# An attention and feed-forward kernel: the tail's exponentials turned through DRAM together with the fourth tile's, decay tiles spread by VectorE from a table, Q and K in one load

## The chip, the core and the metric

One core of a Trainium2 chip runs the whole program in one launch. The metric is the device time of one execution in microseconds (us); lower is better. Three executions of the kernel before are given, and one execution was profiled.

## What is computed

The reference is causal attention with a multiplicative decay, for 8 batches and 8 heads of 576 positions and width 64, and behind it a feed-forward layer of width 2048 with a leaky activation. All is in float32.

```
scores = scale * q @ k^T                       # (8, 8, 576, 576)
cum    = cumsum(log(clip(f, 1e-4, 1)), -1)
scores = where(causal, -1e9, scores + cum[..., :, None] - cum[..., None, :])
attn   = exp(scores - max);  attn = attn / (sum(attn) + 1e-9)
x      = (attn @ v) reshaped to (4608, 512)
h      = x @ w_in                              # (4608, 2048)
out    = where(h > 0, h, alpha * h) @ w_out    # (4608, 512)
```

## The kernel before

**Pairs.** The attention goes over 32 pairs n (8 batches, 4 pairs of heads each). A pair has four query tiles of 128 rows, called tile 0 to 3, for each of its two heads, and a *tail*: the last 64 queries of both heads, stacked as one tile of 128 rows by 576 keys. For each piece TensorE makes the scores (`stretch` L604, `tail` L526), VectorE adds the decay and takes the row's minimum (L639, L541), ScalarE takes the exponentials and their sums (L508).

**Turning.** The product with V needs the exponentials with keys on partitions. Tiles 0 to 2 are turned by TensorE: a transposition of 128 by 128 (`blocks` L521) into a PSUM bank, then a copy into an `eT` buffer (L516, L517). The tail is turned the same way: four blocks (L548), two copies of 256 columns (L551) and one more block of 64 columns (L677, L684). Tile 3 is turned so in the pairs below 8. From pair 8 on (`NX`, L30), in the 24 pairs that the code calls *turned*, tile 3 of both heads is stored to DRAM (`ex`, L659), read back by four loads that put the key's 32-row blocks where they belong (`em`, L660), and turned in 32 by 32 blocks by two VectorE instructions (L665) into `eT3`. The last 64 key rows of `eT3` come in another order than V has, so a second copy of V in that order (`vs`, L497) is loaded for them. The product with V (`prods_of` L687) runs behind the scores of tile 2 of the pair that follows.

**Decay tiles.** `Z` and `Zt` hold the cumulated decay of the two heads, the same on every partition. Except for pair 0 they are loaded from DRAM with a broadcast over partitions: two loads of 256 KB and two of 144 KB a pair (L443, L463). GpSimd then adds the causal mask (L447 to L449, L464).

**Splitting.** From pair 4 on (`NN`), Q and K are split by ScalarE and GpSimd into high and low parts (L472, L473) for products in three terms. `w_in` is split in 16 pieces by `split64` (L306) on ScalarE, VectorE and GpSimd, through the buffers `wr` and `wa`.

**Feed-forward.** `ffn1` (L783) makes the hidden layer of one batch as soon as the four pairs of that batch are done: 192 matmuls of 512 columns a batch, 9 batches in all (the tails make the ninth). They fill TensorE between the pieces of attention; in each, ScalarE and VectorE empty the bank (L803, L805) and a store puts it to DRAM. `ffn2` (L951) follows at the end with seven products for eight.

**What sets the order.** The program makes a list of operations with engine, estimated time, key and buffers; `Plan.run` (L115) plays them through a model of the engines once, while the kernel is built, and issues them in that order. On the chip each engine goes through its list in this fixed order. All DMAs but two at the end are issued by SyncE (SP), in its own fixed order. The model takes a DMA's channel time as its KB over 280 (L160).

## Time and profile before

| what | value |
|---|---|
| three executions | 1069.55, 1071.41, 1076.15 us (median 1071.41) |
| the profiled execution, its own time | 1073.41 us |
| its span in the profile | 1071.6 us |
| mean granted TensorE clock | 0.992 |
| busy: TensorE, weight loads | 1054.9, 916.7 us |
| busy: VectorE, ScalarE, GpSimd | 738.6, 675.0, 280.5 us |
| the last block transposition of the attention (L665) starts at | 580.4 us |

PE is TensorE's matmul row, PEld its weight loads, DVE is VectorE, ACT ScalarE, POOL GpSimd, SPq SyncE's queue of DMAs. Rows that group instructions give the line, the engine, the operation, what it writes and reads, the shape and the count, and behind the bar the busy time in us, the mean duration in ns, and the idle time of the engine before them with what ended it. PEclk is the granted clock of TensorE in tenths. PE durations overlap, since matmuls are pipelined: what one costs is read from the start of one to the start of the next.

### The profile page before, as it was taken

Reading aid. Unit: us, or ns where it says so; the run is one execution under the profiler, and the core shown is the slowest. Engines: PE = TensorE matmul, PEld = TensorE weight load, DVE = VectorE, ACT = ScalarE, POOL = GpSimd, SP = SyncE. Lnnn points to the kernel's source line nnn. Section 1 sums busy time; section 2 is a strip of 40 time slices with the busy share of each in tenths; the row PEclk is TensorE's granted clock in tenths of the full one; section 3 lists DMA queues with packets and bytes.
Section 4 is the critical chain, followed back from the end, with each engine's and each line's share of the span. In section 5 each row is a group of like instructions: output and inputs, shape, how many; then the busy total and the mean of one; then the engine's idle time right before and its main releaser. Section 6 shows DMA issues by size and latency. Waiting matters only on the chain.

```text
span 1071.6 us, 22543 instructions
## 1 busy us (share of the span) xinstructions
PE 1054.9 (98%) x8132; PEld 916.7 (86%) x8132; DVE 738.6 (69%) x1680; ACT 675.0 (63%) x1590; POOL 280.5 (26%) x407
## 2 busy tenths in 40 slices
PE   8889989999999999999999999999999999999998
PEld 5678867888888888888788888899999999999998
DVE  6788864555544545545544599779988898989994
ACT  6879877786766766667655375656454554646551
POOL 6578574553433434344221000000000000000000
PEclk9989999999999999999999999999999999999999
DMA  6967778987887986886763666464444443444411
GB/s 181 268 194 235 225 217 232 271 264 238 253 237 214 259 241 203 242 247 212 215 198 129 204 214 225 167 199 139 136 126 132 137 137 120 138 130 126 140 60 40
DMA packets 152441, 202.15 MB, mean 189 GB/s; under 512 B 18930, under 2 KB 89481, under 8 KB 152329
## 3 DMA queue, kind: packets, MB, share of 16 engines
q1 hardware_dynamic: 152041, 200.51, 61.3%
q8 instruction: 64, 1.05, 0.4%
q14 instruction: 48, 0.39, 0.1%
q10 hardware_dynamic: 288, 0.20, 0.1%
HBM read 139.55 MB, written 61.11 MB: 187 GB/s over the span
## 4 chain that ended last, share of the span: by engine, by line
PE 92%; DMA 2%; POOL 2%; DVE 1%; issue 1%; ACT 1%; SPq 0%; DVEq 0%; POOLq 0%
PE bank L332 86%; PE bank L521 5%; DMA Z<-c 2%; PE bank L392 1%; POOL Z L447 1%; DMA wr<-in_w_in_dram 0%; POOL wi L328 0%; POOL Z L448 0%; PE bank L677 0%; DVE eT L516 0%; DVE wa L322 0%; POOL Z L449 0%; ACT e L508 0%; POOL Ql L473 0%; POOL Kl L473 0%
## 5 line engine op out<-in xcount | busy, mean ns | idle before, releaser
L332 PE MATMUL bank<-xx,wi 128*128 128x512 f32 x1728 | 428.4, 397 | 2.3 <-ACT wi L327 1.8
L332 PEld LDWEIGHTS bank<-xx,wi 128*128 128x128 f32 x1728 | 314.4, 188 | 68.7 <-issue 4.8
L805 DVE SCALAR_TENSOR_TENSOR hs<-bank,sa,hs 128x512 f32<-128x512 f32 x96 | 71.2, 743 | 109.9 <-ACT hs L803 109.8
L332 PE MATMUL bank<-wot,xx 128*128 128x256 f32 x1008 | 123.9, 283 | 0.0
L332 PE MATMUL bank<-wi,xx 128*128 128x256 f32 x1008 | 123.9, 283 | 0.0
L332 PEld LDWEIGHTS bank<-wot,xx 128*128 128x128 f32 x1008 | 122.3, 192 | 0.0
L332 PEld LDWEIGHTS bank<-wi,xx 128*128 128x128 f32 x1008 | 122.3, 192 | 0.0
L508 ACT ACTIVATE e<-e,st 128x512 f32<-128x512 f32 (+2 forms) x160 | 109.2, 685 | 4.2 <-DVE st L541 2.0
L803 ACT ACTIVATE hs<-bank,ab 128x512 f32<-128x512 f32 x96 | 66.0, 688 | 63.4 <-PE bank L332 62.6
L517 ACT ACTIVATE eT<-bank 128x384 f32<-128x384 f32 (+2 forms) x192 | 83.3, 461 | 34.7 <-PE bank L332 20.1
L725 POOL TENSOR_TENSOR xx<-xs,xx 128x256 fp32r<-128x256 f32 x64 | 49.0, 783 | 136.6 <-ACT xx L723 136.4
L473 POOL TENSOR_TENSOR Ql<-rq,Qh 128x640 fp32r<-128x640 f32 x28 | 45.1, 1611 | 137.8 <-ACT Qh L472 89.7
L332 PE MATMUL bank<-eT,vr 128*64 128x128 f32 (+2 forms) x1408 | 80.0, 263 | 0.2 <-DVE eT L516 0.2
L332 PEld LDWEIGHTS bank<-eT,vr 128*64 128x64 f32 x1408 | 63.9, 138 | 14.1 <-issue 7.1
L447 POOL TENSOR_TENSOR Z<-Z,tri 128x384 f32<-128x384 f32 x64 | 60.0, 945 | 45.5 <-DMA Z<-c 31.2
L999 ACT ACTIVATE xx<-gx 128x1024 fp32r<-128x1024 f32 x48 | 50.8, 1058 | 30.8 <-PE bank L332 15.1
L521 PEld LDWEIGHTS bank<-ident,e 128*128 128x128 f32 x384 | 46.9, 146 | 20.5 <-issue 5.3
L521 PE MATMUL bank<-ident,e 128*128 128x128 f32 x384 | 62.2, 287 | 1.9 <-DVE st L639 1.6
L1002 DVE TENSOR_TENSOR xx<-gx,xx 128x1024 fp32r<-128x1024 f32 x48 | 58.6, 1220 | 7.4 <-ACT xx L999 7.4
L332 PE MATMUL bank<-wi,gh 128*128 128x256 f32 x504 | 62.4, 283 | 0.0
L332 PE MATMUL bank<-wot,gh 128*128 128x256 f32 x504 | 62.4, 283 | 0.0
L332 PEld LDWEIGHTS bank<-wot,gh 128*128 128x128 f32 x504 | 61.4, 192 | 0.1
(140 smaller groups left out, 1777.6 us busy)
## 6 DMA issues: line engine op xcount, KB each, us to landing
hd<-hs SPq DMA_DIRECT2D x144, 256.0 KB
wx<-hd SPq DMA_DIRECT2D x47, 512.0 KB
Z<-c SPq DMA_DIRECT2D x62, 256.0 KB
hr<-hd SPq DMA_DIRECT2D x25, 512.0 KB
ex<-e SPq DMA_DIRECT2D x24, 512.0 KB
em<-ex SPq DMA_DIRECT2D x96, 128.0 KB
rq<-in_qq_dram SPq DMA_DIRECT2D x32, 320.0 KB
vr<-in_vv_dram SPq DMA_DIRECT2D x32, 320.0 KB
```

What stands on the lines that cost most here:

```text
L332: pe.matmul(o, lhsT, rhs, start=start, stop=stop)
L392: op("PE", 800, lambda: [pe.matmul(bw.t, wbf[:, 0:128], wbf, start=True, stop=True) for _ in range(3)], -200, [o_wbf], [bw])
L447: m1 = op("POOL", c_po(128 * 3), lambda z4=z4: po.tensor_tensor(z4()[:, 6:9], z4()[:, 0:3], tb(3), ALU.add), kc + 0.1, got + [o_mask], [bZ])
L473: o2 = op("POOL", c_po(w), lambda hi=hi, lo=lo, raw=raw: po.tensor_tensor(lo(), raw.t, hi().bitcast(F32), ALU.subtract), kc, [o1], [raw, bQ])
L508: ex = op("ACT", c_exp(w), lambda: ac.activation(at(bt.t)[:, :w], at(bt.t)[:, :w], AF.Exp, bias=lo()[:, col : col + 1], scale=-1.0, accum_ ...
L517: return op("ACT", c_act(w), lambda: ac.activation(dst(), src(), AF.Copy), key, deps, [bank] + bufs)
L521: pe.transpose(t[:, c : c + 128], src[:, 128 * j : 128 * j + 128], ident)
L725: xl = op("POOL", c_po(256), lambda r=r, t0=t0: po.tensor_tensor(bx.t[:, 1, t0 : t0 + 256], bxs[r].t[:, 0:256], bx.t[:, 0, t0 : t0 + 256]. ...
L803: cp = op("ACT", c_act(512), lambda bh=bh, bs=bs, fc=fc: ac.activation(bs.t, bh.t, AF.Relu, scale=ab[:, fc : fc + 1]), -1000, [last, o_sg] ...
L805: cp = op("DVE", c_dve(512), lambda bh=bh, bs=bs, fc=fc: ve.scalar_tensor_tensor(bs.t, bh.t, sa[:, fc : fc + 1], bs.t, ALU.mult, ALU.add), ...
L999: his.append(op("ACT", c_acs(128 * GW * (j1 - j0)), lambda j0=j0, j1=j1, src=src, o_=o_: ac.activation(o_(0, j0, j1), src(), AF.Copy), key ...
L1002: rdy.append(op("DVE", c_dve(128 * GW * (j1 - j0)), lambda j0=j0, j1=j1, src=src, o_=o_: ve.tensor_tensor(o_(1, j0, j1), src(), o_(0, j0, ...
```

## The change

Three things are done together.

1. **Turned pairs** are now 9 to 31. In them the tail's exponentials are written behind tile 3's in the same buffer, go to DRAM with them in one store (768 KB), come back in the same four loads (12 blocks in place of 8 each), and are turned by two more VectorE instructions. `eT3` has a row of 192 columns for each head and block: 128 of tile 3 and 64 of the tail, so four V matmuls a head of 192 columns take the place of four of 128 and four of 64. The tail's four TensorE transpositions and two copies are gone in these pairs; its last block of 64 columns stays. V comes as one load of eight blocks (`vt`) in place of `vv` and `vs`. Pair 8 turns its tile 3 by TensorE again.
2. **Decay tiles** of pairs 10 to 31 (`NZ`) are no longer loaded. After `w_in` is split, its buffers are free: the 64 rows of the cumulated decay are loaded there once, turned by four VectorE instructions into a table with positions on 32 partitions, copied to the other 96 partitions by six DMAs, and sorted by GpSimd. From the table, two VectorE instructions a pair (1024 and 576 columns) write `Z` and `Zt`, with the same value repeated over 32 columns at their source, so that the turned block has it on every partition. `em` lies in the same memory, and can be used only once the table is made.
3. **Q and K** are one tensor, loaded by one DMA of 608 KB from pair 4 on. The planner's model takes 220 in place of 280 for a DMA's channel time in its first 90 us.

The diff, cut to its core:

```diff
-NX = (8, B * NP)
+FAR = 90.0
+NX = (9, B * NP)
+NZ = 1+9
+NQ = 4
...
-                self.chan = max(self.chan, s + 1.4) + o.kb / 280.0
+                self.chan = max(self.chan, s + 1.4) + o.kb / (220.0 if s < FAR else 280.0)
...
-    rT3 = ring(sp, 1, [128, 2, 4, 128], F32, "eT3_")
-    rm3 = ring(sp, 1, [128, 8, 128], F32, "em")
+    rT3 = ring(sp, 1, [128, 4, 384], F32, "eT3_")
+    wr = sp.tile([128, 1280], U64, name="wr")
+    wf = wr.bitcast(F32)
+    rm3 = Ring(Store([]))
+    em = wf[:, 0:1536].rearrange("p (k s) -> p k s", s=128)
...
-        l_q = op("SP", 450, lambda: sy.dma_start(bq.t, qq[b, p]), kq, dq, [bq], kb=320)
-        l_k = op("SP", 450, lambda: sy.dma_start(bk.t, kk[b, p]), kq, dq, [bk], kb=288)
+        l_qk = [op("SP", 450, lambda c0=c0, c1=c1: sy.dma_start(bqk.t[:, c0:c1], qk[b, p][:, c0:c1]), kq, dq, [bqk], kb=(c1 - c0) / 2)
+                for c0, c1 in (((0, QW), (QW, QW + S)) if n < NQ else ((0, QW + S),))]
...
+        if spread:
+            def rows_of(src, k):
+                return src.rearrange("p s (h o) -> p h s o", o=1).broadcast_to([128, k, src.shape[1], 32])
+
+            zz = op("DVE", c_tr(1024), lambda: ve.transpose(
+                Z()[:, :, 0:512].rearrange("p h (s c) -> p h s c", c=32), rows_of(cq[:, 0:16, 2 * n : 2 * n + 2], 2)), kl + 4, [o_cq], [bZ])
+            zt = op("DVE", c_tr(S), lambda: ve.transpose(
+                Zt().rearrange("p (s c) -> p s c", c=32), rows_of(ct[:, :, n : n + 1], 1)[:, 0]), kl + 4.1, o_ct, [bZ])
...
-            nt = expo(bt, S, 4, st + 0.6, [prev])
+            nt = expo(bt, S, 4, st + 0.6, [prev], tail_of)
+            if turned:
+                return bt, nt
...
-                o_ = op("SP", 400, lambda: sy.dma_start(d.rearrange("h q k -> q h k"), b3.t), key, [be[0][3][1], nm], [b3], kb=512)
+                o_ = op("SP", 400, lambda: sy.dma_start(d.rearrange("g q k -> q g k"), b3.t[:, 0:1536].rearrange("p (g k) -> p g k", g=3)),
+                        key, [be[0][3][1], nm, nt], [b3], kb=768)
...
+                for g in range(3):
+                    def turn(g=g):
+                        o = bT3.t[:, :, 192 * g : 192 * g + 128].rearrange("p s (a c) -> p a s c", a=4) if g < 2 else None
+                        if g < 2:
+                            ve.transpose(o, bm.t[:, 4 * g : 4 * g + 4].rearrange("p a (s r) -> p a s r", r=32))
+                        else:
+                            for h_ in range(2):
+                                ve.transpose(bT3.t[:, :, 192 * h_ + 128 : 192 * h_ + 192].rearrange("p s (a c) -> p a s c", a=2),
+                                             bm.t[:, 8 + 2 * h_ : 10 + 2 * h_].rearrange("p a (s r) -> p a s r", r=32))
...
+    o_cl = op("SP", 400, lambda: sy.dma_start(cl, c8), kc_, [o_c8] + [o for v in w_ready.values() for o in v], kb=147)
...
+    o_qc = [op("SP", 400, lambda a=a, c=c: sy.dma_start(c[32 * a : 32 * a + 32], c[0:32]), kc_ + 2, o_tc, kb=128) for a in range(1, 4) for c in (cq, cq2)]
```

**On TensorE**, a turned pair before. `ident` marks a transposition (L521), `Kh,Qh` and the like are scores, `xx,wi` is the feed-forward layer, `eT` with `vr` or `vs` is the product with V.

```order
L332 MATMUL bank_83<-xx,wi 128x512 x6
L332 MATMUL bank_78<-xx,wi 128x512 x6
L521 MATMUL bank_85<-ident,e_125 128x128 x4
L332 MATMUL bank_82<-xx,wi 128x512 x6
L332 MATMUL bank_84<-Kh_97,Qh_95 128x384
L332 MATMUL bank_80<-Kh_97,Qh_95 128x384
L332 MATMUL bank_84<-Kl_98,Qh_95 128x384
L332 MATMUL bank_80<-Kl_98,Qh_95 128x384
L332 MATMUL bank_84<-Kh_97,Ql_96 128x384
L332 MATMUL bank_80<-Kh_97,Ql_96 128x384
```

The same place in the change, in the first turned pair:

```order
L342 MATMUL bank_79<-xx,wi 128x512 x6
L342 MATMUL bank_82<-xx,wi 128x512 x6
L342 MATMUL bank_81<-Kh_97,Qh_95 128x384
L342 MATMUL bank_83<-Kh_97,Qh_95 128x384
L342 MATMUL bank_81<-Kl_98,Qh_95 128x384
L342 MATMUL bank_83<-Kl_98,Qh_95 128x384
L342 MATMUL bank_81<-Kh_97,Ql_96 128x384
L342 MATMUL bank_83<-Kh_97,Ql_96 128x384
L342 MATMUL bank_84<-eT__114,vr_110 64x128 x6
L342 MATMUL bank_84<-eT_0_115,vr_110 64x192 x6
L342 MATMUL bank_84<-eT_1_118,vr_110 64x64 x2
L342 MATMUL bank_84<-eT_0_115,vr_110 64x192 x2
```

The four transpositions of the tail (`e_125`) are gone, and eight matmuls of 192 columns stand among the V products.

**On TensorE, at pair 10**, the first whose decay tile comes from the table in the change. Before, between the turning of tile 2 and the tail's scores (`128x288`):

```order
L521 MATMUL bank_80<-ident,e_127 128x128 x3
L677 MATMUL bank_80<-ident,e_125 64x128
L521 MATMUL bank_82<-ident,e_126 128x128 x3
L332 MATMUL bank_78<-xx,wi 128x512 x6
L332 MATMUL bank_84<-Kh_97,Qh_95 128x288
```

In the change:

```order
L549 MATMUL bank_78<-ident,e_121 128x128 x3
L342 MATMUL bank_84<-xx,wi 128x512 x6
L342 MATMUL bank_81<-xx,wi 128x512 x6
L618 MATMUL bank_83<-ident,st_129 18x128
L342 MATMUL bank_78<-xx,wi 128x512 x6
L342 MATMUL bank_81<-xx,wi 128x512 x6
L342 MATMUL bank_78<-xx,wi 128x512 x6
L342 MATMUL bank_84<-xx,wi 128x512 x12
L342 MATMUL bank_83<-xx,wi 128x512 x12
L342 MATMUL bank_81<-xx,wi 128x512 x6
L342 MATMUL bank_78<-Kh_97,Qh_95 128x288
```

Sixty feed-forward matmuls stand ahead of the tail's scores of pair 10, where six stood before.

**On SP, the same stretch** in the change; `wr<-c` is the load of the cumulated decay, the copies `wr<-wr` and `sel<-sel` spread the table over the partitions, `wr<-ex` is the load that was `em`:

```order
L865 DMA wr<-c_59 64x576
L516 DMA vr_109<-in_vt_dram 128x1024
L694 DMA ex_63<-e_0_122 128x3x512
L874 DMA wr<-wr 32x1024
L874 DMA sel<-sel 32x128
L874 DMA wr<-wr 32x1024
L874 DMA sel<-sel 32x128
L874 DMA wr<-wr 32x1024
L874 DMA sel<-sel 32x128
L853 DMA hd<-hs 128x512
```

In pairs 10 to 31 the rows of L443 and L463 are no longer on SP; `vr` and `vs` are one row there.

**On VectorE, in pair 3's tail**, before. L318 to L323 split a piece of `w_in`, L721 divides by the sums and waits for a load, L541 takes the tail's minimum.

```order
L318 TENSOR_SCALAR wa_145<-wr_144 128x512
L319 SCALAR_TENSOR_TENSOR wa_145<-wr_144,wa_145 128x512
L516 COPY eT_0_120<-bank_84 128x512
L516 COPY eT_0_120<-bank_78 128x512
L583 RECIPROCAL st_135<-st_135 128x9
L322 SCALAR_TENSOR_TENSOR wa_145<-wr_144,wa_145 128x512
L323 SCALAR_TENSOR_TENSOR wa_145<-wi,wa_145 128x512
L721 TENSOR_TENSOR xs_1_137<-xs_1_137,ri_140 128x256
L721 TENSOR_TENSOR xs_1_139<-xs_1_139,ri_140 128x320
L541 ISA e_125,st_133<-bank_85,Zt_110 128x288
```

In the change:

```order
L571 ISA e_119,st_127<-bank_79,Zt_108 128x288
L571 ISA st_127 128x1
L544 COPY eT_0_115<-bank_85 128x4x128
L616 RECIPROCAL st_129<-st_129 128x9
L544 COPY eT_0_115<-bank_84 128x4x128
L328 TENSOR_SCALAR wr<-wr 128x512
L329 SCALAR_TENSOR_TENSOR wr<-wr 128x512
L332 SCALAR_TENSOR_TENSOR wr<-wr 128x512
L333 SCALAR_TENSOR_TENSOR wr<-wi,wr 128x512
L767 TENSOR_TENSOR xs_1_131<-xs_1_131,ri_134 128x256
L767 TENSOR_TENSOR xs_1_133<-xs_1_133,ri_134 128x320
L571 ISA e_119,st_127<-bank_78,Zt_108,st_127 128x288
```

The first half of the minimum (L541, now L571) moved ahead of the piece of `w_in`; the second half still stands behind the division.

## Prediction

> **What bounds the kernel now.** I read the page's busy shares and slices first, then the stretches, then TensorE's waits.

> ```profile
> PE 1054.9 (98%) x8132; PEld 916.7 (86%) x8132; DVE 738.6 (69%) x1680; ACT 675.0 (63%) x1590; POOL 280.5 (26%) x407
> PE 92%; DMA 2%; POOL 2%; DVE 1%; issue 1%; ACT 1%; SPq 0%; DVEq 0%; POOLq 0%
> ```

> TensorE is busy for 98% of the span and makes 92% of the chain that ended last. The page warns that pipelined matmuls look busy, so the stretches come next (PE, PEld, DVE, ACT, POOL busy, then granted clock, DMA share, GB/s).

> ```profile
> 30.00:60.00 30.00, 27.16 (x238) 19.72 (x236) 26.60 (x77) 25.62 (x75) 19.13 (x27) 0.89 0.84 244
> 60.00:90.00 30.00, 26.64 (x229) 21.95 (x228) 24.79 (x57) 22.48 (x64) 22.17 (x28) 0.89 0.66 207
> 150.00:180.00 30.00, 26.92 (x186) 20.53 (x185) 16.77 (x39) 23.10 (x65) 20.15 (x26) 1.00 0.85 245
> 180.00:570.00 390.00, 390.00 (x3115) 315.38 (x3113) 197.85 (x596) 270.21 (x746) 158.60 (x224) 1.00 0.79 232
> 570.00:700.00 130.00, 130.00 (x669) 107.66 (x669) 89.10 (x157) 72.94 (x121) 3.92 (x4) 1.00 0.57 192
> 700.00:1071.60 371.60, 367.71 (x3046) 366.69 (x3044) 322.34 (x589) 190.78 (x332) 0.00 (x0) 1.00 0.40 126
> ```

> From 180 us to the output TensorE never idles: 390 of 390, 130 of 130. In the attention the feed-forward matmuls fill whatever is left, and what isn't done then is done behind it. So a microsecond of TensorE work taken out of a pair there comes off the end, as long as nothing new makes TensorE wait. VectorE is half busy there (198 of 390), ScalarE 69%, the DMA engines 79%. TensorE's idle time lies elsewhere, and its waits name it (us in total, times, longest).

> ```profile
> PE bank L521 <- DVE st L541: 2.6, 1, 2.6
> PE bank L585 <- DVE st L583: 1.9, 1, 1.9
> PE bank L332 <- ACT wi L327: 1.8, 1, 1.8
> PE bank L521 <- DVE st L639: 1.6, 1, 1.6
> PE bank L332 <- ACT R L586: 1.5, 1, 1.5
> ```

> Idle is 16.7 us in all (1071.6 - 1054.9); these five are 9.4 of it, all before 180 us, where the clock too is granted at 0.89 for a while.

> **The change part by part.**

> *Transpositions.* In 23 turned pairs the tail's four blocks leave TensorE: 92. Pair 8 gets back eight (two heads of tile 3). Net 84 fewer. What one costs is read from starts:

> ```profile
> 119.35 2.93 PE L332 MATMUL bank<-xx,wi 128*128 128x512 f32 x12
> 122.11 0.82 PE L521 MATMUL bank<-ident,es 128*128 128x128 f32 x6
> 122.86 0.45 PE L332 MATMUL bank<-Kh,Qh 64*128 64x384 f32 x2
> ...
> 126.92 1.64 PE L332 MATMUL bank<-xx,wi 128*128 128x512 f32 x6
> 128.39 1.04 PE L521 MATMUL bank<-ident,e 128*128 128x128 f32 x8
> 129.35 0.33 PE L332 MATMUL bank<-Kh,Qh 64*128 64x128 f32 x2
> ```

> Six take 122.86 - 122.11 = 0.75, eight take 0.96: 0.12 each. Some of that is the change from one kind of work to the next, so bounds of 0.105 and 0.125 stand: 8.8 to 10.5 us. I take 0.115: **-9.7**.

> The group row of all 384 says the same by another way: 62.2 us busy, 0.162 each, with overlaps to the next kind of work in it; its mean duration of 287 ns is a latency.

> ```profile
> L521 PE MATMUL bank<-ident,e 128*128 128x128 f32 x384 | 62.2, 287 | 1.9 <-DVE st L639 1.6 <-ACT e L508 0.2
> ```

> [...]

> *V products.* Four of 128 columns and four of 64 a head become four of 192: the same columns, eight instructions fewer a pair. No row has 192 columns. The upper bound for the gain is from the records of 64 columns:

> ```profile
> 246.49 1.04 PE L332 MATMUL bank<-eT,vs 128*64 128x128 f32 x16
> 247.37 1.40 PE L332 MATMUL bank<-eT,vr 128*64 128x64 f32 x28
> 248.70 3.02 PE L332 MATMUL bank<-xx,wi 128*128 128x512 f32 x12
> ```

> Sixteen records of 128 take 0.88, 0.055 each. The next 28 take 1.33; four in them have 256 columns and four 128, at 0.11 and 0.055 that is 0.66, which leaves 0.034 for each of 20 with 64 columns, 0.006 over half of 0.055. Sixteen such overheads a pair are 0.1 us, 2.4 in all. If the wider ones cost as much more, the loss would be as much: -2.4 to +2.4. Streaming is the nearest row, so I take **-0.5**.

> *ScalarE* loses two copies of 385 ns a pair, 0.77, and has 31% idle: nothing.

> *VectorE* gains work. The nearest rows are its own block transposition and what waits before it:

> ```profile
> L665 DVE STREAM_TRANSPOSE eT<-em 128x512 f32<-128x512 f32 x48 | 32.0, 693 | 42.5 <-DMA em<-ex 17.8 <-DMA rq<-in_qq_dram 7.3 <-PE bank L332 6.5
> L517 ACT ACTIVATE eT<-bank 128x256 f32<-128x256 f32 x56 | 18.5, 385 | 4.9 <-PE bank L521 4.9
> ```

> 512 columns take 0.69. By columns, 1024 take 1.4, 576 take 0.78, twice 256 take 0.8 with the fixed part; a source that repeats one value is not in the trace: I take the price by columns, with twice that as the upper bound. 22 x 2.2 + 23 x 0.8 = 67 us, nearly all of it in 180 to 570 us: VectorE goes from 51% to about 67%, or 84% at twice the price. The cover is its idle time, 192 us; it costs nothing unless an instruction that TensorE waits for comes to stand behind a late one. That is the PV chain.

> *The PV chain.* Store, four loads, two turns, then the V product. For one pair (SP, then VectorE, then TensorE):

> ```profile
> 371.93 0.39 SPq L659 DMA_DIRECT2D ex<-e  x1
> ...
> 377.89 0.38 SPq L660 DMA_DIRECT2D em<-ex  x1
> 378.37 0.87 SPq L443 DMA_DIRECT2D Z<-c  x2
> 379.29 1.09 SPq L463 DMA_DIRECT2D Zt<-c  x2
> 380.43 1.57 SPq L660 DMA_DIRECT2D em<-ex  x3
> ```

> ```profile
> 388.36 0.71 DVE L665 STREAM_TRANSPOSE eT<-em 128x512 f32<-128x512 f32 x1 [3.84 <-DMA rq<-in_qq_dram]
> ...
> 389.62 0.70 DVE L665 STREAM_TRANSPOSE eT<-em 128x512 f32<-128x512 f32 x1
> ```

> ```profile
> 390.57 0.88 PE L332 MATMUL bank<-eT,vr 128*64 128x128 f32 x12
> ```

> The second turn ends at 390.32 and the product starts at 390.57: the order is tight, and VectorE stood 3.84 us for the landing. The change adds 256 KB to the store and as much to the loads, at 232 GB/s 1.1 us each, and 0.8 us of turns: +3.0. It takes away the two Z and two Zt loads, 800 KB, that here stood between the `em` loads: -3.4. The order was also made with these sizes in it. So I take the chain as no later, **0**, with bounds of a little below nothing and +2 us in half the pairs.

> *Loads.* SP issues a Q and K load less (28 pairs), a V load less (23) and four decay loads less (22). The DMA engines carry about 350 KB a pair less (800 of decay and 64 of V gone, 512 of turning added). That is off TensorE's path: 0. Q must now wait for K's landing too, but splits stand ahead of their scores by several feed-forward runs.

> *The table.* One load, four turns, six copies, four GpSimd copies, then the first decay tile; VectorE waits for the copies, with feed-forward evictions behind it, and TensorE's tail scores of pair 10 wait for banks. Landings in that stretch:

> ```profile
> SPq L598 <- DMA rd<-R: 35.0, 14, 3.9
> 127.04 6.68 DMA Z<-c
> 143.95 7.71 DMA Z<-c
> ```

> A small one takes 2.5 us, a crowded one 7.7. Two in turn are 5 to 15; with some 2 us of VectorE, 3 of issues and 3 of GpSimd the table takes 13 to 23. The sixty feed-forward matmuls moved ahead of it cover 60 x 0.230 = 13.8 (0.230 is 2.76 / 12, from the rows at 119.35). So the loss is 0 to 9 us; the middle of the DMA rows, with other work overlapping, gives **+1.5**.

> *Early pairs.* In pair 3 the first half of the tail's minimum (L541) now stands ahead of a `w_in` piece on VectorE, so the 2.6 us wait above should shrink; the second half, and with it 1.9 and 1.5, stay behind a division that waits for a load. 0 to -7, below it also some +3, if the longer Q and K load delays a split: **-1.5**.

> **Sum.** -9.7 - 0.5 + 1.5 - 1.5 = -10.2. The profiled execution took 1073.4 (span 1071.6, 1.8 around it): it comes to 1063.2. The median of the runs is 2.0 lower, 1071.4, and so the forecast for it is 1071.4 - 10.2 = 1061.2, say **1061**.

> **The rivals.**

> *The early waits vanish* (chance 0.15). The five waits above go, and with them half of what the clock costs. At 0.89 over 60 us some 6 us of full speed are missing. -10.2 with -7 in place of -1.5 and 0 for the table: about 1054. For it: less DMA and another order. Against it: VectorE is busy 26.6 of 30 there, so the waits have a second cause.

> *The table is late* (0.14). +9 in place of +1.5: 1069, no change that can be told. For it: two landings in a row, where one took 7.7. Against it: the order leaves 13.8 us.

> *The turned chain is late in most pairs* (0.11), slower than before. One `em` and one `eT3` buffer, half as much again to move, VectorE's turns four in place of two. If in half of the pairs the product with V starts 2 us late, that is 12 x 2 = 24 us, which TensorE cannot fill since its order is fixed: 1061 + 24 = 1085. It eats the gain from 0.45 us a pair on (10.2 / 23). For it: 0.25 us of slack in the rows above. Against it: 800 KB fewer in the way.

> *A transposition costs its latency* (0.03). Then 84 x 0.287 = 24 us go in place of 9.7: 1047. The starts speak against it. [...]

> *TensorE's work falls, and the end doesn't move* (0.02), because another engine sets the pace of the attention: 1071. The 390 of 390 speak against it.

> **How the numbers follow.** The forecast has 0.55 and its own range is 1057 to 1066. About 1% (10.7 us) is what a measurement of this kernel can tell from no change, so faster means below 1060.7: just under half of the forecast (0.26), the early rival and the latency, 0.44. Slower means above 1082: 0.11. The same: 0.45. The range reaches down to 1052 for the early rival and up to 1075 for a late table, and leaves out the slower case and the latency.

> **What would show it.** Right: TensorE's busy time falls by about 10 us with 300 transpositions of `e` in place of 384; it stays without idle from 200 us on; VectorE's share in 180 to 570 us goes to about two thirds, and L443 has 18 loads. A row `PE <- DVE eT` of many times in TensorE's waits would show the chain late; one long wait near 160 to 180 us, the table. The forecast is wrong if TensorE's busy time falls by less than 8 us, or if its idle time grows by more than 5.

## The result, and the profile after

The changed kernel took 1057.63 us (median of 4 runs, 1056.91 to 1059.07), the kernel before 1071.72 beside it: a ratio of 0.9865, with a 95% interval of 0.9832 to 0.9898. That is 14.1 us less, where the prediction's terms add up to 10.2 less; the time lies 0.6 us above the lower end of the forecast's range (1057 to 1066). Run again beside the experiments (e5), it gave 1057.48 against 1072.56, a ratio of 0.9861 (0.9841 to 0.9881). The profiled execution took 1056.91, its span is 1054.7.

The page's busy shares, and the chain that ended last:

```profile
PE 1041.1 (99%) x7680; PEld 901.6 (85%) x7680; DVE 797.8 (76%) x1772; ACT 661.7 (63%) x1546; POOL 283.6 (27%) x411
PE 96%; DVE 2%; POOL 1%; ACT 0%; issue 0%; DVEq 0%
```

TensorE is busy for 13.8 us less than before (1054.9), and idle for 13.6 in place of 16.7. Not all of the 13.8 is work that left it: in the traces' records of the granted clock, the kernel before stands at half rate for 17.1 us of its first 71 us, the changed kernel for 10.2. Half of the difference, 3.4 us, is the clock's part, an estimate from the 0.50 that was granted there (50.3 to 57.1 us before); 10.4 are left. The same stretches as in the prediction (PE, PEld, DVE, ACT, POOL busy, clock, DMA share, GB/s) tell where:

```profile
30.00:60.00 30.00, 26.10 (x227) 18.96 (x226) 27.43 (x69) 24.38 (x70) 20.62 (x27) 0.89 0.88 261
60.00:90.00 30.00, 27.06 (x239) 22.04 (x238) 24.64 (x61) 23.10 (x64) 22.44 (x29) 0.94 0.58 181
150.00:180.00 30.00, 30.00 (x206) 24.83 (x205) 20.52 (x53) 20.17 (x56) 17.94 (x28) 1.00 0.75 215
180.00:570.00 390.00, 390.00 (x2774) 310.73 (x2773) 256.04 (x692) 265.26 (x726) 160.63 (x224) 1.00 0.76 219
700.00:1054.70 354.70, 351.05 (x2926) 350.84 (x2924) 309.91 (x569) 180.09 (x315) 0.00 (x0) 1.00 0.39 120
```

From 180 to 570 us TensorE still never idles, VectorE went from 51% to 66% (256 of 390). The idle 3.1 us at 150 to 180 are gone. At 30 to 90 us nothing was won: 6.8 us idle (60 - 26.10 - 27.06), where it was 6.2. TensorE's waits agree, all of them before 64 us; the 1.8 us behind ScalarE's `wi` isn't there any more:

```profile
PE bank L342 <- DVE st L571: 2.3, 1, 2.3
PE bank L618 <- DVE st L616: 1.9, 2, 1.3
PE bank L549 <- DVE st L674: 1.6, 1, 1.6
PE bank L342 <- ACT R L619: 1.6, 1, 1.6
```

The groups of the added and the reduced work (busy us, mean ns of one, idle before):

```profile
L549 PE MATMUL bank<-ident,e 128*128 128x128 f32 x300 | 48.3, 285 | 2.7 <-DVE st L674 1.6 <-ACT e L536 1.0
```

```profile
L453 DVE STREAM_TRANSPOSE Z<-wr 128x1024 f32<-128x1024 f32 x22 | 27.4, 1244 | 0.7
L706 DVE STREAM_TRANSPOSE eT<-wr 128x256 f32<-128x256 f32 x46 | 17.0, 407 | 0.0
L455 DVE STREAM_TRANSPOSE Zt<-sel 128x576 f32<-128x576 f32 x22 | 16.7, 758 | 0.0
```

There are 300 transpositions of `e`, as forecast. The spread, whose price no row of before showed, costs 1.24 and 0.76 us, a little under the price by columns that was taken (1.4 and 0.78). It lies on the line of the dense turnings (0.407 us for 256 columns here, 0.69 for 512 before), so a source that repeats one value shows no price of its own.

### The profile page after: what moved, and what is told of

Read it like the earlier page. It is cut to its first block, busy times and chain, and to the rows that moved or that the text cites. A ratio compares the mean times of both kernels' runs of the same rounds, so it can differ in the third digit from the quotient of the medians.

```text
span 1054.7 us, 21382 instructions
## 1 busy us (share of the span) xinstructions
PE 1041.1 (99%) x7680; PEld 901.6 (85%) x7680; DVE 797.8 (76%) x1772; ACT 661.7 (63%) x1546; POOL 283.6 (27%) x411
## 3 DMA queue, kind: packets, MB, share of 16 engines
HBM read 125.41 MB, written 66.61 MB: 182 GB/s over the span
## 4 chain that ended last, share of the span: by engine, by line
PE 96%; DVE 2%; POOL 1%; ACT 0%; issue 0%; DVEq 0%
PE bank L342 90%; PE bank L549 5%; PE bank L402 1%; PE bank L718 0%; DVE wr L332 0%; DVE wr L329 0%; DVE xs L767 0%; PE bank L618 0%; DVE wr L333 0%; DVE e L674 0%; POOL Z L469 0%; ACT es L536 0%; DVE eT L544 0%; DVE eT__114 L544 0%; POOL wi L338 0%
## 5 line engine op out<-in xcount | busy, mean ns | idle before, releaser
L536 ACT ACTIVATE e<-e,st 128x384 f32<-128x384 f32 (+2 forms) x127 | 84.8, 672 | 2.9 <-issue 1.1
L1073 ACT ACTIVATE xx<-gx 128x1024 fp32r<-128x1024 f32 x48 | 50.8, 1058 | 30.6 <-PE bank L342 12.7
L342 PE MATMUL bank<-eT,vr 128*64 128x192 f32 (+3 forms) x896 | 69.3, 303 | 0.0
L1076 DVE TENSOR_TENSOR xx<-gx,xx 128x1024 fp32r<-128x1024 f32 x48 | 58.5, 1219 | 8.2 <-ACT xx L1073 8.2
L342 PEld LDWEIGHTS bank<-eT,vr 128*64 128x64 f32 x896 | 55.1, 137 | 8.1
L342 PEld LDWEIGHTS bank<-wi,gh 128*128 128x128 f32 x504 | 61.3, 192 | 0.0
L755 ACT ACTIVATE xs<-bank 128x320 f32<-128x320 f32 (+1 forms) x64 | 25.5, 409 | 56.9 <-PE bank L342 29.3
L497 POOL TENSOR_TENSOR Ql<-rqk,Qh 128x640 fp32r<-128x640 f32 x28 | 45.4, 1620 | 57.4 <-ACT Qh L496 44.5
L342 PE MATMUL bank<-Kh,Qh 64*128 64x128 f32 (+1 forms) x280 | 60.4, 365 | 0.0
```

The costliest lines, as they stand in the source:

```text
L342: pe.matmul(o, lhsT, rhs, start=start, stop=stop)
L497: o2 = op("POOL", c_po(w), lambda hi=hi, lo=lo, raw=raw: po.tensor_tensor(lo(), raw(), hi().bitcast(F32), ALU.subtract), kc, [o1], [bqk, bQ])
L536: ex = op("ACT", c_exp(w), lambda: ac.activation(at(bt.t)[:, :w], at(bt.t)[:, :w], AF.Exp, bias=lo()[:, col : col + 1], scale=-1.0, accum_ ...
L755: xs_ops[r].append(op("ACT", c_act(w_), lambda: ac.activation(bxs[r].t, bP.t[:, 0:w_], AF.Copy), st, [pvo], [bP, bxs[r]]))
L1073: his.append(op("ACT", c_acs(128 * GW * (j1 - j0)), lambda j0=j0, j1=j1, src=src, o_=o_: ac.activation(o_(0, j0, j1), src(), AF.Copy), key ...
L1076: rdy.append(op("DVE", c_dve(128 * GW * (j1 - j0)), lambda j0=j0, j1=j1, src=src, o_=o_: ve.tensor_tensor(o_(1, j0, j1), src(), o_(0, j0, ...
```

## The experiments

Times are medians, and a ratio is to runs of the kernel before beside the run. Unless it is said otherwise, a difference is against the changed kernel run again (e5, 1057.48). Only e6 to e8 ran beside e5. By the ratios, e2, e10 and e12 come out 0.7 to 1.7 us lower than by the medians, and the others within 0.4 us. Each ratio is known to some 1.5 to 2 us either way, so a difference of two to some 2.5.

The traces are sharper. In e1, e2, e3, e7, e8 and e10 the order of TensorE is that of the changed kernel up to 98 us at least. So the time from one matmul behind the early waits to the end of the last matmul can be compared: 1051.05 - 85.65 = 965.40 us in the changed kernel.

```profile
85.65 0.44 PE L342 MATMUL bank<-Kh,Qh 64*128 64x384 f32 x2
...
1041.77 9.28 PE L342 MATMUL bank<-wi,xx 128*128 128x256 f32 x76
```

In e5 it is 965.42, although e5 reaches this matmul 0.5 us earlier. Between these two executions of one kernel, the difference lies wholly in the early stage.

**e1: the removed transpositions put back, alone.** In `tail`, for turned pairs:

```diff
             if turned:
+                bTt = Buf(rT)
+                op("PE", 4 * 109, lambda: blocks(bTt.t, 0, tail_of(bt.t), range(4)), st + 1.3, [nt, o_id], [bTt, bt])
                 return bt, nt
```

> The changed kernel, but in its 23 turned pairs TensorE turns the tail's four blocks as well, into a bank that nobody reads: 92 transpositions added, nothing else taken back (the turns through DRAM stay). If the gain is TensorE's instructions that left, each at the 0.11 us from start to start of such a group, the time rises by 92 x 0.109 to 0.115 = 10.0 to 10.6 us over the changed kernel, to about 1068. If a transposition costs its latency of 0.285 us: +26 us. If the gain came from the lighter DMA queues or the new order and TensorE has room: 0 to +2.

1068.19 us; ratio to before 0.9962 (0.9948 to 0.9976). That is +10.7, or 0.116 us for each of the 92, give or take 0.03. No new wait came with them, and TensorE's busy time rose:

```profile
PE 1053.2 (99%) x7772; PEld 913.4 (86%) x7772; DVE 797.9 (75%) x1772; ACT 662.8 (62%) x1546; POOL 282.7 (26%) x411
```

The rise of 12.1 us has 3.4 of the clock in it: this execution stands at half rate for 17.1 us early, as the kernel before, in the changed kernel's own order. Behind the early waits the trace gives the price alone:

```profile
87.74 0.44 PE L342 MATMUL bank<-Kh,Qh 64*128 64x384 f32 x2
...
1054.74 8.56 PE L342 MATMUL bank<-wi,xx 128*128 128x256 f32 x70
```

1063.30 - 87.74 = 975.56 against 965.40: 10.16 us, 0.110 for each. The price by starts holds, the latency (+26) and "TensorE has room" (0 to +2) don't. The 84 that the change took away are worth 84 x 0.110 = 9.3 us; 0.116 would make it 9.8.

**e2: the product with V in 128 and 64 columns again.**

```diff
-both.append(head + [(j + 4, 128, 320, t3[:, j]) for j in range(3)] + [(3, 256, 320, ...)] + [(7, 128, 320, t3[:, 3])])
+both.append(head + [(j + 4, 128, 256, t3[:, j, 0:128]) for j in range(4)]
+            + [(j + 4, 256, 320, t3[:, j, 128:192]) for j in range(4)] + [(3, 256, 320, ...)])
```

> The changed kernel with its product with V issued as before in the turned pairs: four instructions of 128 and four of 64 columns a head in place of four of 192, from the same tiles, the order otherwise the same. 23 x 8 = 184 instructions more, the same columns. By the prediction's term +0.5 us; by the stretches between feed-forward runs (3.851 us a pair before, 3.798 after) 23 x 0.053 = +1.2; if every small instruction has an overhead of its own, up to +2.4. A rise of 3 us or more would make this a main cause of what the prediction missed.

1059.34 us; ratio 0.9870 (0.9848 to 0.9891): +1.9 (+1.0 by the ratios), inside the noise of the two but on the expected side. One product in the changed kernel, to the start of what follows:

```profile
378.35 0.88 PE L342 MATMUL bank<-eT__114,vr 128*64 128x128 f32 x12
379.06 2.24 PE L342 MATMUL bank<-eT,vr 128*64 128x192 f32 x28
381.22 0.96 PE L342 MATMUL bank<-xx,wi 128*128 128x512 f32 x3
```

and in e2:

```profile
380.68 0.88 PE L342 MATMUL bank<-eT__114,vr 128*64 128x128 f32 x12
381.39 2.28 PE L342 MATMUL bank<-eT,vr 128*64 128x128 f32 x44
383.60 1.66 PE L342 MATMUL bank<-xx,wi 128*128 128x512 f32 x6
```

381.22 - 378.35 = 2.87 against 2.92: 0.05 a pair, 1.2 us in 23 pairs. Over the whole stretch behind the early waits e2 takes 966.27 us, 0.9 more than the changed kernel.

**e3: decay tiles loaded again** (`NZ = 99`; the table is still made, and not used).

> The changed kernel, but with the decay tiles of pairs 10 to 31 loaded by DMA as before (four loads and 800 KB a pair) in place of VectorE's spreading; the tail is still turned through DRAM. The table is still made and not used. If the gain is TensorE's work and both chains have cover: 0, within 1.5 us. If the lighter queues carry the gain, or if the turned chain has no slack when 800 KB stand in its way again (3.4 us a pair at 232 GB/s): +3 at least, and up to +24 with waits of TensorE for the turned tiles. VectorE's share from 180 to 570 us would fall from 66% to about 55%.

1062.75 us; ratio 0.9909 (0.9888 to 0.9929): +5.3. It looks as if the lighter queues carried a third of the gain, but the pairs themselves lost nothing: 390 of 390 again, at a DMA share of 0.92. The loss stands in one place behind the attention:

```profile
180.00:570.00 390.00, 390.00 (x2741) 311.40 (x2741) 218.39 (x644) 259.64 (x709) 157.60 (x222) 1.00 0.92 260
```

```profile
694.00:698.00 4.00, 1.09 (x9) 0.89 (x8) 4.00 (x6) 2.54 (x4) 0.00 (x0) 0.99 0.97 278
698.00:701.40 3.40, 3.40 (x18) 3.40 (x18) 3.37 (x8) 0.25 (x1) 0.00 (x0) 0.50 0.96 312
```

TensorE idles 2.9 us for `xx` of VectorE (L1076) at the start of `ffn2`, and then runs 3.4 us at half its clock: 4.6 us together. Behind the early waits the whole trace is 4.2 us longer than the changed kernel's (969.58), so this place is the loss. It isn't the price of the 800 KB a pair either: e12 loads the same and has no wait there. The planner made another order here; that this order is the cause is not shown apart.

**e4: the planner's rate of 280 throughout** (`FAR = 0`).

> The changed kernel with the planner's one channel rate of 280 at all times, as before, in place of 220 for the first 90 us: nothing but the order changes, and with it the early order comes back to that of before (the scores ahead of the transpositions at pair 2 and 3). If the order that this constant gives has removed the 3.5 us of TensorE's waits at 147 to 176 us, or part of the clock's loss, the time rises by 2 to 5 us. If not, 0 within 1.5.

1062.95 us; ratio 0.9909 (0.9887 to 0.9931): +5.5. One wait of 1.46 us at 146 us came, for ScalarE's exponentials (`es`) and not for `wi`. Its early stage stands at half rate for 13.7 us, where e5's has 10.2: another 1.7. The remaining 2.3 us the trace doesn't place. So the constant isn't what took the waits for `wi` away.

**e5: the changed kernel again.**

> The changed kernel itself, nothing edited, as the yardstick on the same chip for the runs beside it. By the ratio measured before, 0.9865 of the kernel before: 1057 to 1059 us.

1057.48 us, as said above.

**e6: the planner's constant alone, in the kernel before.**

```diff
-self.chan = max(self.chan, s + 1.4) + o.kb / 280.0
+self.chan = max(self.chan, s + 1.4) + o.kb / (220.0 if s < 90.0 else 280.0)
```

> The kernel before with one line of the change alone: the planner counts 220 in place of 280 for a transfer's rate in the first 90 us. No instruction is added or removed, only the order differs. If this constant by itself brings the 5 us that its removal cost the changed kernel (early waits, and the 3.5 us of waits at 147 to 176 us): about 1067. If the waits at 147 to 176 us went because pairs 8 to 11 have less to move and no mask tiles to turn, the constant does nothing here: within 2 us of before.

1069.89 us; ratio to before 0.9977 (0.9962 to 0.9992), 2.7 less than before (0.9 to 4.1). That is between the two figures, and the interval reaches the second: some early waits went, but the wait for `wi` stands (2.00 us at 149 us), and a new one of 1.64 us came at 327 us.

**e7: every Z spread twice** (the same `ve.transpose` issued two times).

> The changed kernel, but VectorE writes each decay tile Z twice (22 more instructions of 1.24 us, 27 us of its time), and the planner doesn't know. By the prediction VectorE's idle time covers it: 0 within 1.5 us, no wait of TensorE after 200 us. If VectorE's work were on the path, up to 27 us; in half of the pairs a wait of 1.2 us behind it: +13.

1058.91 us; ratio 0.9873 (0.9854 to 0.9893): +1.4, against 27 us of added work.

```profile
180.00:570.00 390.00, 389.48 (x2772) 310.07 (x2771) 281.38 (x714) 266.07 (x730) 160.42 (x224) 1.00 0.76 219
```

VectorE is at 72% and cost one wait of 0.5 us (at 181 us); behind the early waits the trace is 0.8 us longer than the changed kernel's (966.24). The cover is there.

**e8: two waits put into the attention.** In the reduction of tile 2's scores (L674):

```diff
+for _ in range(1 + ({15: 6, 21: 10}.get(n, 0) if (h, i) == (0, 2) else 0)):
     ve.tensor_tensor_reduce(...)
```

> The changed kernel, but VectorE does one reduction of the third tile's scores six times more in pair 15 (3.8 us at 0.63 each) and ten times more in pair 21 (6.3 us), with the same result, and the planner doesn't know: it puts one short and one longer wait of TensorE into the attention, where it otherwise never waits. The transpositions of that tile start some 3.5 us after its exponential ends, so TensorE should idle 0 to 1 us at pair 15 and 2 to 4 us at pair 21. If a wait costs only itself: the time rises by the idle. If the half-rate stretches of the clock that stand about 3 us behind TensorE's waits of 1.3 to 2.9 us in the traces follow from these waits: one stretch of 3.4 or 6.8 us at half rate behind pair 21's wait, and the time rises by 1.7 to 3.4 us more than the idle; none behind a wait below 1 us.

1061.08 us; ratio 0.9894 (0.9872 to 0.9916): +3.6. Pair 15's repeats were covered wholly. At pair 21 TensorE waited once, not for the transposition but for the next scores' bank:

```profile
385.42 0.39 PE L342 MATMUL bank<-Kh,Qh 64*128 64x512 f32 x1
387.55 0.50 PE L342 MATMUL bank<-Kh,Qh 64*128 64x512 f32 x1 [1.74 <-DVE st L675]
...
389.25 2.91 PE L342 MATMUL bank<-xx,wi 128*128 128x512 f32 x6
```

```profile
385.80:387.50 1.70, 0.01 (x1) 0.00 (x0) 1.63 (x7) 0.00 (x0) 0.00 (x0) 1.00 0.75 227
387.50:389.20 1.70, 1.65 (x12) 1.18 (x13) 1.67 (x4) 1.64 (x6) 0.00 (x0) 0.99 0.04 9
389.20:392.60 3.40, 3.40 (x12) 2.82 (x11) 3.15 (x15) 2.88 (x8) 3.20 (x3) 0.51 0.00 0
392.60:396.00 3.40, 3.40 (x20) 2.83 (x19) 3.08 (x8) 3.20 (x12) 2.70 (x5) 1.00 0.49 100
```

The wait of 1.74 us has a stretch of 3.4 us at half clock behind it, in which six matmuls take 2.91 us in place of 1.66. Half of 3.4 is 1.7: with the wait 3.4, and the run is 3.6 longer (3.8 by the trace behind the early waits, 969.21). The wait cost double.

**e9: pair 8 turned too** (`NX = (8, ...)`, `NZ = 9`).

> The changed kernel with one pair more turned: pair 8 as well, and so the table made one pair earlier and the decay tiles spread from pair 9 on. Twelve transpositions fewer, at the 0.116 us each that the added ones cost: -1.4 us, and -0.1 for its product with V. If the table has its cover also one pair earlier: 1056. If the conversions of w_in hold the table's memory so long that pair 9 waits for its decay tile: a wait of TensorE of 2 to 9 us near 140 to 170 us, and a time of 1058 to 1066.

1065.36 us; ratio 0.9931 (0.9917 to 0.9944): +7.9, though 12 more transpositions are gone. TensorE's waits in two windows, 150 to 157 us and 236 to 250:

```profile
PE bank L342 <- ACT wi L337: 2.0, 1, 2.0
```

```profile
PE bank L342 <- ACT eT L725: 1.5, 1, 1.5
PE bank L342 <- DVE eT L706: 0.9, 1, 0.9
PE bank L549 <- ACT es L536: 0.7, 2, 0.5
```

The first, behind the conversions of `w_in`, has a half-rate stretch behind it. The second group has the turned chain in it, the only late one of all runs: `DVE eT L706`. Five waits of 5.1 us and 1.7 for the clock are 6.8 of the 9.4 that are to be explained (7.9 + 1.5). The wait of 2.0 us came where the expectation put one for the table's memory, but it is for `wi`; none is put down to a decay tile.

**e10: the rate of 220 for 120 us** (`FAR = 120`).

> The changed kernel with the planner's rate of 220 kept for the first 120 us in place of 90: the order is the same up to pair 5 (some 75 us) and differs behind it. If 220 is simply the better figure while the queues are full, the time stays at 1057 or falls by 1. If the constant's worth is which single waits an order happens to leave, some other wait comes or goes: anything from 1056 to 1063, with any rise standing as one to two waits of 1 to 3 us and a half-rate stretch behind them.

1060.87 us; ratio 0.9886 (0.9872 to 0.9900): +3.4 (+2.7 by the ratios). One wait of 1.7 us for a copy of ScalarE came at 243 us, and no half rate behind it. Behind the early waits the trace is 2.2 us longer than the changed kernel's (967.57); what the medians show above that lies within their noise. So 220 isn't simply the better figure.

**e11: Q and K as two loads** (`NQ = 99`).

> The changed kernel with Q and K as two loads in all 32 pairs, as before, in place of one from pair 4 on: 28 more loads, the same bytes. By the prediction the joined load is worth nothing: 0 within 1.5 us, no wait of TensorE for a split (Qh, Kh, Ql, Kl). The planner makes a new order behind pair 3, so a rise by single waits, as in the runs before, is the rival: up to +5.

1060.84 us; ratio 0.9890 (0.9876 to 0.9904): +3.4. No split is waited for. TensorE waits 4.1 us for a reciprocal of nine columns that the new order put behind three pieces of VectorE, the first two parts of a conversion; 10.2 us at half rate follow (64.1 to 74.3), where the changed kernel has 3.4:

```profile
61.82 1.61 DVE L328 TENSOR_SCALAR wr<-wr 128x512 uint32<-128x512 uint32 x1 [0.61 <-POOL wi L338]
63.47 1.10 DVE L329 SCALAR_TENSOR_TENSOR wr<-wr 128x512 uint32<-128x512 uint32 x1
64.49 0.68 DVE L544 COPY eT<-bank 128x512 f32<-128x512 f32 x1
65.09 0.20 DVE L616 RECIPROCAL st<-st 128x9 f32<-128x9 f32 x1
```

In the changed kernel it stands ahead of them, at 61.41.

**e12: all three of those parts undone at once** (`NZ = 99`, `NQ = 99`, `FAR = 0`).

> The changed kernel with its three other parts undone together: decay tiles loaded by DMA (e3), Q and K as two loads in all pairs (e11), one channel rate of 280 (e4). What is left is the tail turned with the fourth tile and the product with V in 192 columns (and the table, made and not used). If the parts are additive, each with a worth of its own, their prices add up: 1057.5 + 5.3 + 5.5 + 3.4 = 1071.7, no faster than before. If each price was only what the new order happened to leave in single waits, and TensorE's removed work is the whole reliable gain: 1072.4 - 9.8 - 1.9 = 1060.7, give or take 3 for such waits.

1057.38 us; ratio to before 0.9844 (0.9825 to 0.9863), the same as the changed kernel's 0.9861 within their noise. Single prices of 5.3, 5.5 and 3.4 add up to nothing.

```profile
180.00:570.00 390.00, 390.00 (x2772) 311.19 (x2771) 219.31 (x647) 261.61 (x718) 157.93 (x224) 1.00 0.91 262
```

```profile
HBM read 143.43 MB, written 66.61 MB: 199 GB/s over the span
```

The core reads 18 MB more than the changed kernel (125.41), the DMA engines are at 91%, VectorE is back at 56%, and TensorE doesn't idle.

## Why the prediction was right, and where it was off

The direction, and the mechanism that carries most of it, were right: TensorE sets the pace (busy for 390 of 390 us from 180 to 570, before and after), and the work taken from it came off the end. That the sum came near is in part luck: the table's term was 4.6 us too pessimistic and the early pairs' 2.1 too hopeful, and the two partly cancel.

- *Transpositions*: -9.7 forecast, -9.3 by e1's trace (-9.8 by its medians). Right, and the latency rival (24 us) falls.
- *V products*: -0.5 forecast, -0.9 by e2's trace (-1.2 by the starts of one product). The price by columns was the right side; what eight instructions fewer a pair bring at the same columns, 0.05 us by the starts (2.92 to 2.87), was taken too low.
- *ScalarE, VectorE, loads*: 0 each. e7 shows VectorE's cover: 27 us of added work cost 0.8 us behind the early waits. e12 shows that decay loads, joined loads and the constant together are worth nothing here, within the noise.
- *The PV chain*: 0, right. In e3 and e12 it has 800 KB a pair in its way again, and TensorE waits nowhere from 180 to 570 us. Of the rival (1085) the runs show one wait of 0.9 us, in e9.
- *The table*: +1.5 forecast. This is the step that failed. The table had its cover (load issued at 155.2, first spread at 169.4, 14 us, no wait):

```profile
L865 SPq DMA_DIRECT2D wr<-c x1: 450/450/450, 155.2 to 155.2; - x1
```

```profile
L453 DVE STREAM_TRANSPOSE Z<-wr x22: 1232/1245/1249, 169.4 to 517.9; 128x1024 f32<-128x1024 f32 x22
```

  And the stretch around it, in which before idled for 3.1 us (26.92 of 30), has no wait left. The prediction counted pair 8's return to TensorE as eight transpositions more and took no wait from it. The three kernels that turn pair 8 while `w_in` is still being split (before, e6, e9) wait 1.8, 2.0 and 2.0 us for ScalarE's `wi`; the others (the changed kernel, e1 to e5, e7, e8 and e10 to e12) have no such wait. Spreading from the table isn't what removed it, since e3 and e12 load their decay tiles. e9 makes its table a pair earlier as well, so the runs don't take this apart further, and why the order comes out so is open.
- *Early pairs*: -1.5 forecast, +0.6 in TensorE's idle time. The minimum of pair 3 did move, and the wait moved with it: 2.3 us for its second half in place of 2.6. The prediction put the second half's delay down to the division and its load. In the trace the division (L767) begins without a wait and takes 0.82 us, and what stands ahead is the piece of `w_in`: 5.6 us from 43.86 to 49.45. Its second instruction takes 2.08 us here, where the median of L329 is 0.69; why is open. The rival of 1054, in which the early waits vanish, isn't what happened.

```profile
43.86 0.42 DVE L328 TENSOR_SCALAR wr<-wr 128x512 uint32<-128x512 uint32 x1
44.31 2.08 DVE L329 SCALAR_TENSOR_TENSOR wr<-wr 128x512 uint32<-128x512 uint32 x1
46.43 1.78 DVE L332 SCALAR_TENSOR_TENSOR wr<-wr 128x512 uint32<-128x512 uint32 x1
48.24 1.28 DVE L333 SCALAR_TENSOR_TENSOR wr<-wi,wr 128x512 f32<-128x512 f32 x1
49.45 0.82 DVE L767 TENSOR_TENSOR xs<-xs,ri 128x256 f32<-128x256 f32 x2
50.18 0.51 DVE L571 CUSTOM_DVE_ANT_0 e<-bank,Zt,st 128x288 f32<-128x288 f32 x1
```

- *Sum*: -9.3 - 0.9 - 3.1 + 0.6 = -12.7, against -14.1 and -15.1 by the medians. The two profiled executions' spans are 16.9 apart, of which 3.4 is the clock: together 16.1, and 0.8 isn't placed. The clock's part isn't a gain of the change. In the changed kernel's own early order the profiled executions of e5, e2 and e1 stand at half rate for 10.2, 13.7 and 17.1 us, so it belongs to the execution. How much of it is in the medians isn't known.

What the prediction didn't see at all is how much a new order can cost by itself. e3, e4 and e11 each undo something that e12 shows to be worth nothing, and each is 3.4 to 5.5 us slower; e10, which only moves the constant's end, 3.4, and e9 7.9. For e10 and e11 that is little more than the noise, but their traces show the waits. Where the trace shows the reason it is one to five single waits and the clock behind them, in places that have little to do with the edit. That the rest of this change comes to nothing is therefore a statement about two orders, the changed kernel's and e12's, that both happen to leave no wait behind 90 us. Where e4's remaining 2.3 and e9's remaining 2.6 us lie is open, and so is whether an order without the early waits exists: none of the runs has one, and none is faster than the changed kernel by more than its noise.

## What to carry to other kernels

Where one engine is busy in every stretch, count the instructions that leave it, at the distance from start to start in the trace; that gave 9.7 us here, where the trace of e1 shows 9.3, while the DMA traffic, the second engine's load and the loads' number, all much changed, were worth nothing together. With a static order, price each edit also by the waits that a new order may bring: undoing parts one at a time gave 5.3, 5.5 and 3.4 us, and undoing them together gave 0, so single ablations across a planner must not be added up. Look for such waits in the trace before giving an edit credit for its time, and where the order is the same, compare the stretch behind the early waits: it agreed to 0.02 us between two executions whose starts differed by 0.5.

## What the runs showed of the hardware

A wait of TensorE cost double in e8: 1.74 us of wait with 3.4 us at half the clock behind it, in a run 3.6 us longer. These traces have nine waits of 1.4 us or more behind 90 us. Behind five (2.91 us in e3, 2.00 and 1.64 in e6, 1.97 in e9, 1.74 in e8) the granted clock goes to 0.5 for 3.4 us, beginning 0.6 to 1.6 us after the wait's end; behind four (1.83 before, 1.71 in e10, 1.49 in e9, 1.46 in e4) it doesn't. So 1.64 us was enough in e6, where 1.83 before had no half rate behind it: the length alone doesn't decide.

VectorE's 32 by 32 turning with a source that repeats one value 32 times took 1.24 us for 1024 columns, where 256 and 512 dense ones take 0.41 and 0.69; carried on in a line, these two give an estimate of 1.26. So spreading the table over the partitions in this way had about the price of a plain turning.
